# Squared-ReLU attention with a top-1 expert layer: another order of pairs in one chunk, later writes of transposed blocks, earlier v loads, two casts on another engine

## The chip, the cores and the metric

One core of a Trainium2 chip. The metric is the device time of one execution of the whole kernel in microseconds (us), as the median of several runs. Engines are named as the profile names them: PE (TensorE), DVE (VectorE), ACT (ScalarE), POOL (GpSimd) and SP (SyncE, whose queue issues nearly all DMAs here).

## The reference

Eight batches of 2496 tokens, 256 wide; z is 64 wide. Attention without a softmax, then a top-1 expert layer in which each of 8 experts takes at most 80 tokens.

```python
scores = (1.0 / S) * np.matmul(z, z.transpose(0, 2, 1))
attn = np.maximum(scores, 0.0) ** 2
x = (u * np.matmul(attn, v)).reshape(B * S, D)
logits = x @ w_gate                       # softmax, argmax: expert and gate weight of a token
...
h = np.maximum(x[tok_idx] @ w1[e], 0.0)   # the 80 tokens of largest gate weight for each expert
out[tok_idx] = gate_w[tok_idx, None] * (h @ w2[e])
```

The scores are symmetric: the block of rows i and columns j is the transpose of the block (j, i).

## The kernel before

The 2496 tokens of a batch are padded to NT = 20 tiles of 128. Four tiles make a chunk of 512 (NQ = 5 chunks), two tiles make a pair (NP = 10 pairs of keys). A step is one (batch b, query chunk qc, pair r): 50 steps for a batch, 400 in all, in the list `steps`. Chunks and pairs count from 0.

**A step on PE.** `attend` (L332) multiplies the 512 scores of two key tiles with v and accumulates over all pairs of the chunk in two PSUM banks (`acc`): for each tile and each half of D three matmuls, with v and the scores split in a high and a low part (L343 to L345); the last, half-filled tile k = 19 needs two (L347, L348). That makes 12 matmuls for a pair, 10 for the pair 9. `start` is given at k = 0, `stop` at the last tile.

**Where a step's scores come from.** `scores` (L303) is named LOOK = 2 steps ahead of `attend`. Either it computes them, when the key chunk is not below the query chunk: four matmuls (L312, L313) into PSUM, ReLU and square on ACT (L316, L317), the high part `ah` as a cast on ACT or DVE (`cp`, L105 or L107: DVE in the diagonal blocks and for the (chunk, tile) pairs in `ON_V`, from batch 1 on), the low part `al` as a subtraction on DVE (L54). Or, when the key chunk j is below the query chunk i, it takes the block (i, j) that an earlier chunk has computed, transposed (`mirrored`, L283): then ACT casts (L296) and DVE subtracts from a tile `blk`. Each chunk so begins with 2 qc mirrored pairs and ends with computed ones.

**How a block is mirrored.** `mirror` (L252) transposes 32 x 32 pieces of a computed tile on DVE into x (L257; four buffers), and after a block's fourth tile names the write of x to DRAM, y<-x (L261). `mirror_back` (L265), called at the end of each step, names the four reads blk<-y (L278) of the next block in the order of use, when its write is two or more steps back, its use is at most AHEAD = 12 steps away and one of NA = 4 slots is free. `to_read` holds each block's use step.

**What sets the order.** The order on PE, ACT, DVE and SP is the order in which the code names the instructions; each engine takes its own in that order. A DMA on SP that waits, for data or for a free buffer, holds all that is named after it on SP. In a step the order is: x of the finished chunk (at r = 0), `scores` of two steps ahead, v's preparation in batch 0, `attend`, `finished` (the rest for the chunk before: high, middle and low parts of x, its DMA transposes xq L412, its store xs L421 and L426, logits, gates), then the loads: z of the next batch (L100) at r = 1, the swapped z (zd, L120 and L121) at r = 1, u at r = 2, zeros to the output (L236) at r = 5, v (L132, two raw buffers), in batch 7 the expert weights (`weights_ahead`), at last `mirror_back`.

**v of the next batch.** Its groups 0 and 1 are loaded at pair 8 of chunk 3. In chunk 4, at pairs 2, 4, 6, 8 and 9, `prep_v` splits a group (cast on ACT L105, subtraction on DVE L146) and the load of the group after next is named. In batch 0 the same is done within chunk 0 at pairs 0, 2, 4 and 6.

After the attention comes the expert stage (from L798 on), which the change does not touch.

Of the kernel before, what the change touches and what calls it, by code (L numbers as in the profile page):

```python
# [8 lines left out]
F32 = mybir.dt.float32  # L9
# [16 lines left out]
def attn_moe_kernel(ctx, tc, zT, uT, v, wg, w1, w2, out, seq, cap):  # L26
# [5 lines left out]
    nc = tc.nc  # L32
    V = nc.vector
    B, _, SP = zT.shape
# [3 lines left out]
    NT = SP // P  # L38
# [3 lines left out]
    QT = 4  # L42
    NQ = NT // QT
# [9 lines left out]
    def tt(o, a, b, op):  # L53
        V.tensor_tensor(out=o, in0=a, in1=b, op=op)  # L54
# [9 lines left out]
    dram = ctx.enter_context(tc.tile_pool(name="dram", bufs=1, space=DRAM))  # L64
# [3 lines left out]
    SQ = 32  # L68
# [58 lines left out]
    def load_v(b, g):  # L127
        last = g == NQ - 1
        nf = QT - 1 if last else QT
        raw = zpool.tile([P, QT, D], F32, tag="vraw", name=f"vraw_{b}_{g}")  # L130
        r0 = g * CH
        nc.sync.dma_start(out=raw[:, :nf],  # L132
                          in_=v[b, r0:r0 + nf * P, :].rearrange("(t p) d -> p t d", p=P))
        if last:

            r1 = r0 + nf * P
            for h in range(2):
                nc.sync.dma_start(out=raw[h * 64:(h + 1) * 64, nf], in_=v[b, r1:r1 + TAIL, :])
        return raw
# [93 lines left out]
    def zero_out(i, n):  # L233
# [3 lines left out]
                          in_=zero.rearrange("p (o d) -> p o d", o=1).broadcast_to([P, r1 - r0, D]))  # L237


    LOOK, AHEAD = 2, 12  # L240
    a_t = {}

# [1 line left out]

    half_t, y_t, blk, slot_of, free = {}, {}, {}, {}, list(range(NA))
    n32 = P // SQ
    now = [0]

    to_read = [(b, i, j, ((b * NQ + i) * NT + j * QT) // 2 - LOOK)
               for b in range(B) for i in range(NQ) for j in range(i)]  # L250

    def mirror(b, i, j, t, a):  # L252

        if t == 0:
            half_t[b, i, j] = sqpool.tile([P, n32, QT, QT, SQ], F32, tag="x", name=f"x_{b}_{i}_{j}")
        x = half_t[b, i, j]
        V.transpose(out=x[:, :, :, t].rearrange("p n k s -> p k n s"), in_=a)  # L257
        if t < QT - 1:
            return
        y = dram.tile([n32, SQ, n32, QT * QT * SQ], F32, tag="y", name=f"y_{b}_{i}_{j}", bufs=12)  # L260
        nc.sync.dma_start(out=y.rearrange("g p h f -> (g p) (h f)"),  # L261
                          in_=x.rearrange("p h k t s -> p (h k t s)"))
        y_t[b, i, j] = y, now[0]

    def mirror_back():  # L265

# [15 lines left out]
    def pair_tile(tag, b, qc, k, dt=F32R, bufs=3):  # L282
        return ew.tile([P, 2, CH], dt, tag=tag, name=f"{tag}_{b}_{qc}_{k}", bufs=bufs)  # L283
# [17 lines left out]
    def scores(b, qc, k):  # L301

        if k // QT < qc:  # L303
            return mirrored(b, qc, k)
        nq = min(CH, seq - qc * CH)
        zc, zd = zc_t[b, qc], zd_t[b, qc]
        a = pair_tile("a", b, qc, k, F32, 2)
        ss = []
        for h in range(2):
            zk = zc_t[b, k // QT][:, (k % QT + h) * P:(k % QT + h + 1) * P]  # L310
            s = ps_s.tile([P, CH], F32, tag="s", name=f"s_{b}_{qc}_{k + h}")
            nc.tensor.matmul(s[:, :nq], zk, zc[:, :nq], start=True, stop=False)  # L312
            nc.tensor.matmul(s[:, :nq], zk, zd[:, :nq], start=False, stop=True)  # L313
            ss.append(s)
        for h, s in enumerate(ss):
            nc.scalar.activation(out=a[:, h, :nq], in_=s[:, :nq], func=AF.Relu)  # L316
        nc.scalar.activation(out=a[:, :, :nq], in_=a[:, :, :nq], func=AF.Square)  # L317
        ah = pair_tile("ah", b, qc, k)
        on_v = k // QT == qc or (qc, k) in ON_V and b > 0
        cp(V if on_v else nc.scalar, ah[:, :, :nq], a[:, :, :nq])  # L320
        al = pair_tile("al", b, qc, k)
        tt(al[:, :, :nq], a[:, :, :nq], ah[:, :, :nq], ALU.subtract)
        if k // QT > qc:
            for h in range(2):
                mirror(b, k // QT, qc, k % QT + h, a[:, h])
        a_t[b, qc, k] = (ah, al)
# [2 lines left out]

    def attend(b, qc, k, cols=range(DC)):  # L330
        nq = min(CH, seq - qc * CH)
        if k == 0:  # L332
            acc_t[b, qc] = [ps_a.tile([P, CH], F32, tag="acc", name=f"acc_{b}_{qc}_{c}")
                            for c in range(DC)]
        acc = acc_t[b, qc]
        ah, al = (x[:, k % 2, :nq] for x in a_t[b, qc, k - k % 2])
        vt = v_t[b, k // QT]
        t = k % QT
        for c in cols:
            cs = slice(c * P, (c + 1) * P)  # L340
            o = acc[c][:, :nq]
            if k < NT - 1:
                nc.tensor.matmul(o, vt[:, t, 0, cs], ah, start=k == 0, stop=False)  # L343
                nc.tensor.matmul(o, vt[:, t, 1, cs], ah, start=False, stop=False)  # L344
                nc.tensor.matmul(o, vt[:, t, 0, cs], al, start=False, stop=False)  # L345
            else:
                nc.tensor.matmul(o, vt[:, t, 0, cs], ah, start=False, stop=False)  # L347
                nc.tensor.matmul(o, vt[:, t, 0, cs], al, start=False, stop=True)  # L348


    xt_t, xq_t, lg_t = {}, {}, {}
# [256 lines left out]
        ts(pre["half"], incl[:, :, NBLK - 3], -15.5, ALU.add)  # L608


    NP = NT // 2

    ON_V = {(0, 8), (0, 12), (0, 16)}

    early = [(e, w, part) for e in range(2) for w in (1, 2) for part in range(2)]
    qa, qb, qz = NQ - 3, NQ - 2, NQ - 1
# [4 lines left out]
    WARM = 4, 12  # L621
    steps = [(b, qc, r) for b in range(B) for qc in range(NQ) for r in range(NP)]
    ET = mybir.EngineType
    v_raw, z_raw, w_raw = {}, {}, {}
# [68 lines left out]
    with tc.manual_schedule(engines={ET.PE, ET.Activation, ET.DVE, ET.SP}):  # L693
        prep_zc(0, 0, raw0)
        prep_zd(0, 0, raw0)
        prep_zc(0, 1, raw12[:, 0])
        scores(0, 0, 0)
        prep_v(0, 0, vraw0, nc.scalar, V)
        scores(0, 0, 2)
        v_raw[0, 1] = vraw1  # L700
        z_raw.update({(0, 2): raw12[:, 1], (0, 3): raw34[:, 0], (0, 4): raw34[:, 1]})
        constants()
        prev = None
        for i, (b, qc, r) in enumerate(steps):
            last = b == B - 1 and qc == NQ - 1
            now[0] = i
            if r == 0 and prev:
                chunk_x(*prev)
            if (b, qc) == (0, 0) and r in (0, 2, 4):
                prep_zc(0, r // 2 + 2, z_raw.pop((0, r // 2 + 2)))  # L710
            if i + LOOK < len(steps):
                nb, nqc, nr = steps[i + LOOK]
                scores(nb, nqc, 2 * nr)
            if b == 0 and qc == 0:
                if r % 2 == 0 and r < 8:
                    g = r // 2 + 1
                    prep_v(0, g, v_raw.pop((0, g)), nc.scalar, V)
                    if g + 1 < NQ:
                        v_raw[0, g + 1] = load_v(0, g + 1)
                if r == 8:  # L720
                    constants_v()
            for k in (2 * r, 2 * r + 1):
                if not last or k < NT - 3:
                    attend(b, qc, k)
            if prev:
                finished(*prev, r)

            nb, nqc = (b, qc + 1) if qc + 1 < NQ else (b + 1, 0)
            if r == 2:
                prep_u(b, qc)  # L730
            if b + 1 < B:
                if r == 1:
                    z_raw[b + 1, qc] = load_z(b + 1, qc)
                if r == 9:
                    prep_zc(b + 1, qc, z_raw.pop((b + 1, qc)))
                if qc == NQ - 2 and r == 8:
                    for g in range(2):
                        v_raw[b + 1, g] = load_v(b + 1, g)
                if qc == NQ - 1:
                    g = (r - 1) // 2 if r < 9 else 4  # L740
                    if r in (2, 4, 6, 8, 9):
                        prep_v(b + 1, g, v_raw.pop((b + 1, g)), nc.scalar, V)
                        if g + 2 < NQ:
                            v_raw[b + 1, g + 2] = load_v(b + 1, g + 2)
            if nb < B and r == 1:
                prep_zd(nb, nqc)
            if r == 5:
                zero_out(b * NQ + qc, B * NQ)
            if b == B - 1 and qc >= NQ - 3:
                weights_ahead(qc, r)  # L750
            mirror_back()
            if r == NP - 1:
                prev = b, qc

        chunk_tiles(*prev)
        for kk, c in ((3, 0), (2, 0), (3, 1), (1, 0), (2, 1), (1, 1)):
            attend(*prev, NT - kk, [c])
            if kk == 1:
                chunk_x_last(*prev, c)
        chunk_store(*prev)  # L760
        chunk_logits_last(*prev)
        gate_top(b, NQ - 1, NQ)
        gate(b, NQ - 1, NQ)
        chunk_store2(*prev)
        kb = B * BPB
        count_last(kb - 2, kb)
        blocks(ps_m, "m", gp, oh, kb - 2, kb)
# [546 lines left out]
```

## Time and profile before

| | |
|---|---|
| median of 3 runs | 1446.32 us (1445.33 to 1446.89) |
| the profiled execution | 1441.15 us, its span 1439.4 us |
| PE busy | 1385.3 us |
| DVE busy | 1074.9 us |
| ACT busy | 983.1 us |
| moved by DMA | 311.98 MB, mean 217 GB/s |
| mean granted clock of PE | 0.991 |

The profile's busy time of an engine is the union of its instructions' times, and a matmul's drawn length is longer than its slot in the pipeline, so that busy PE is not PE at its peak. A timeline row has start, length, engine, line, operation, out<-in, and in brackets the idle time of the engine before it with what ended it. A row of waits has the engine and instruction that waited, what it waited for, the total, the number of times and the longest. A row of windows has a stretch, its length, and the busy time of each engine with its number of instructions. For SP, a row is the time of issuing, not of the transfer. A row of DMA issues ends with the median time from issue to landing.

### The profile page before, as it was taken

How to read it: one execution, taken by the hardware profiler on the slowest of the kernel's cores; microseconds unless marked ns; L12 is line 12 of the kernel's file. 1: busy time of each engine (PE TensorE's matmuls, PEld its weight loads, DVE VectorE, ACT ScalarE, POOL GpSimd, SP SyncE). 2: the span in 40 equal slices, each digit the busy share in tenths (PEclk: the TensorE clock that was granted, in tenths of full speed). 3: DMA queues.
4: the chain of work that ended last, by engine and by line, in shares of the span. 5: the costliest groups of instructions: out<-in, count | busy, mean ns of one | idle time of the engine just before them, and what ended most of it. 6: DMA issues, size and time to landing. Idle time of an engine off the chain costs nothing. (4 is left out here: it accounts for less than half of the span.)

```text
span 1439.4 us, 19509 instructions
## 1 busy us (share of the span) xinstructions
PE 1385.3 (96%) x7086; PEld 1135.8 (79%) x7086; DVE 1074.9 (75%) x1530; ACT 983.1 (68%) x1263; POOL 47.5 (3%) x48
## 2 busy tenths in 40 slices
PE   8999999999999999999999999999999999999687
PEld 6788877888788887888788877888878888887466
DVE  7766788667877688677877678767887678766784
ACT  8776677767776587756676577766776667766264
POOL 0000000000000000000000000000000000000075
PEclk9999999999999999999999999999999999999899
DMA  6799978996999959997899959999598979999944
GB/s 203 207 227 223 242 198 209 239 243 157 236 247 222 251 157 216 263 213 210 232 210 237 241 156 235 240 230 259 152 233 237 240 159 238 235 231 253 207 147 134
DMA packets 300103, 311.98 MB, mean 217 GB/s; under 512 B 136184, under 2 KB 228224, under 8 KB 289760
## 3 DMA queue, kind: packets, MB, share of 16 engines
q1 hardware_dynamic: 299040, 309.11, 86.3%
q0 software_dynamic: 960, 1.56, 0.4%
q8 instruction: 57, 0.93, 0.3%
q14 instruction: 46, 0.38, 0.1%
HBM read 153.48 MB, written 126.46 MB: 194 GB/s over the span
## 5 line engine op out<-in xcount | busy, mean ns | idle before, releaser
L345 PE MATMUL acc<-al,vt 128*128 128x512 f32 (+1 forms) x1520 | 587.5, 386 | 7.3 <-DVE al L54 7.1
L343 PE MATMUL acc<-ah,vt 128*128 128x512 f32 (+1 forms) x1520 | 586.9, 386 | 6.3 <-ACT ah L296 4.0
L344 PE MATMUL acc<-ah,vt 128*128 128x512 f32 (+1 forms) x1520 | 586.0, 386 | 1.2 <-DVE vt L146 1.2
L54 DVE TENSOR_TENSOR al<-a,ah 128x1024 fp32r<-128x1024 f32 (+1 forms) x240 | 291.2, 1213 | 143.8 <-ACT ah L105 134.2
L345 PEld LDWEIGHTS acc<-al,vt 128*128 128x128 f32 x1520 | 285.7, 188 | 66.8 <-DVE al L54 14.4
L343 PEld LDWEIGHTS acc<-ah,vt 128*128 128x128 f32 x1520 | 285.8, 188 | 63.5 <-ACT ah L296 7.4
L344 PEld LDWEIGHTS acc<-ah,vt 128*128 128x128 f32 x1520 | 285.9, 188 | 55.1 <-DVE vt L146 2.0
L316 ACT ACTIVATE a<-s 128x512 f32<-128x512 f32 (+1 forms) x480 | 257.6, 588 | 83.1 <-PE s L313 73.4
L296 ACT CAST ah<-blk 128x1024 fp32r<-128x1024 f32 x160 | 166.9, 1048 | 163.0 <-DMA blk<-y 81.7
L54 DVE TENSOR_TENSOR al<-blk,ah 128x1024 fp32r<-128x1024 f32 x160 | 193.0, 1214 | 93.0 <-ACT ah L296 90.5
L317 ACT ACTIVATE a<-a 128x1024 f32<-128x1024 f32 (+1 forms) x240 | 253.0, 1054 | 7.6
L257 DVE STREAM_TRANSPOSE x<-a 128x512 f32<-128x512 f32 x320 | 207.6, 686 | 0.0
L313 PE MATMUL s<-zd,zc 128*128 128x512 f32 (+1 forms) x480 | 186.9, 389 | 0.0
L105 ACT CAST ah<-a 128x1024 fp32r<-128x1024 f32 x139 | 146.0, 1050 | 4.4
L312 PE MATMUL s<-zc,zc 128*128 128x512 f32 x320 | 131.3, 410 | 3.5 <-ACT a L316 3.4
L107 DVE CAST ah<-a 128x1024 fp32r<-128x1024 f32 (+1 forms) x101 | 68.6, 679 | 46.6 <-ACT a L317 46.6
L313 PEld LDWEIGHTS s<-zd,zc 128*128 128x128 f32 x480 | 90.4, 188 | 15.4 <-issue 0.5
L373 ACT CAST xb<-xf 128x1024 bf16<-128x1024 f32 (+1 forms) x39 | 40.1, 1027 | 57.3 <-DVE xf L362 57.2
L312 PEld LDWEIGHTS s<-zc,zc 128*128 128x128 f32 x320 | 60.1, 188 | 21.8 <-ACT a L316 11.8
L312 PE MATMUL s<-zc 128*128 128x512 f32 (+1 forms) x160 | 63.8, 399 | 7.7 <-ACT a L316 7.6
L146 DVE TENSOR_TENSOR vt<-vraw,vt 128x1024 fp32r<-128x1024 f32 (+1 forms) x40 | 46.7, 1167 | 27.8 <-ACT vt L105 27.6
L105 ACT CAST vt<-vraw 128x1024 fp32r<-128x1024 f32 (+3 forms) x56 | 44.9, 828 | 30.9 <-DMA vraw<-v 30.9
(161 smaller groups left out, 843.3 us busy)
## 6 DMA issues: line engine op xcount, KB each, us to landing
y<-x SPq DMA_DIRECT2D x80, 1024.0 KB, 5.4
blk<-y SPq DMA_DIRECT2D x320, 256.0 KB, 8.3
out<-idle SPq DMA_DIRECT2D x40, 512.0 KB, 9.3
vraw<-v SPq DMA_DIRECT2D x32, 512.0 KB, 8.4
ut<-uT SPq DMA_DIRECT2D x32, 512.0 KB, 5.4
xs<-xq SPq DMA_DIRECT2D x32, 512.0 KB, 7.6
wraw<-w SPq DMA_DIRECT2D x28, 512.0 KB, 6.1
zd<-zc SPq DMA_DIRECT2D x78, 128.0 KB, 3.5
```

Source lines behind the costliest of these rows:

```text
L54: V.tensor_tensor(out=o, in0=a, in1=b, op=op)
L105: eng.copy(out=o, in_=i)
L107: eng.tensor_copy(out=o, in_=i)
L257: V.transpose(out=x[:, :, :, t].rearrange("p n k s -> p k n s"), in_=a)
L296: nc.scalar.copy(out=natural(ah), in_=src)
L312: nc.tensor.matmul(s[:, :nq], zk, zc[:, :nq], start=True, stop=False)
L313: nc.tensor.matmul(s[:, :nq], zk, zd[:, :nq], start=False, stop=True)
L316: nc.scalar.activation(out=a[:, h, :nq], in_=s[:, :nq], func=AF.Relu)
L317: nc.scalar.activation(out=a[:, :, :nq], in_=a[:, :, :nq], func=AF.Square)
L343: nc.tensor.matmul(o, vt[:, t, 0, cs], ah, start=k == 0, stop=False)
L344: nc.tensor.matmul(o, vt[:, t, 1, cs], ah, start=False, stop=False)
L345: nc.tensor.matmul(o, vt[:, t, 0, cs], al, start=False, stop=False)
```

## The change

1. Chunk 3 (the fourth) takes its pairs in the order 8, 9, 0, 1, ..., 7, by a list `pairs_of`. `start` and `stop` of the accumulation, the use steps of the blocks and the look ahead follow that list. So the block (4, 3), which pairs 8 and 9 of chunk 3 compute, is computed first in the chunk.
2. `mirror` no longer names the write y<-x; it notes it, and `mirror_out`, called at the end of each step after `mirror_back`, names it two steps later.
3. The next batch's v groups 0 and 1 are loaded at pairs 2 and 4 of chunk 3 in place of both at pair 8.
4. `ON_V` keeps (0, 8) alone: the casts of chunk 0's tiles 12 and 16 go to ACT, in batches 1 to 7.

```diff
+    NP = NT // 2
+    pairs_of = [list(range(NP)) for qc in range(NQ)]
+    pairs_of[NQ - 2] = [NP - 2, NP - 1, *range(NP - 2)]
...
-    now = [0]
-    to_read = [(b, i, j, ((b * NQ + i) * NT + j * QT) // 2 - LOOK)
+    now, to_write = [0], []
+    to_read = [(b, i, j, (b * NQ + i) * NP + pairs_of[i].index(2 * j) - LOOK)
...
         if t < QT - 1:
             return
-        y = dram.tile([n32, SQ, n32, QT * QT * SQ], F32, tag="y", name=f"y_{b}_{i}_{j}", bufs=12)
-        nc.sync.dma_start(out=y.rearrange("g p h f -> (g p) (h f)"),
-                          in_=x.rearrange("p h k t s -> p (h k t s)"))
-        y_t[b, i, j] = y, now[0]
+        to_write.append((now[0], b, i, j, x))
+
+    def mirror_out():
+        while to_write and to_write[0][0] + 2 <= now[0]:
+            _, b, i, j, x = to_write.pop(0)
+            y = dram.tile([n32, SQ, n32, QT * QT * SQ], F32, tag="y", name=f"y_{b}_{i}_{j}", bufs=12)
+            nc.sync.dma_start(out=y.rearrange("g p h f -> (g p) (h f)"),
+                              in_=x.rearrange("p h k t s -> p (h k t s)"))
+            y_t[b, i, j] = y, now[0]
...
-        if k == 0:
+        first, last = 2 * pairs_of[qc][0], 2 * pairs_of[qc][-1] + 1
+        if k == first:
...
-    ON_V = {(0, 8), (0, 12), (0, 16)}
+    ON_V = {(0, 8)}
...
-                scores(nb, nqc, 2 * nr)
+                scores(nb, nqc, 2 * pairs_of[nqc][nr])
...
-            for k in (2 * r, 2 * r + 1):
+            p = pairs_of[qc][r]
+            for k in (2 * p, 2 * p + 1):
...
-                if qc == NQ - 2 and r == 8:
-                    for g in range(2):
-                        v_raw[b + 1, g] = load_v(b + 1, g)
+                if qc == NQ - 2 and r in (2, 4):
+                    g = r // 2 - 1
+                    v_raw[b + 1, g] = load_v(b + 1, g)
...
             mirror_back()
+            mirror_out()
```

More of the change, by code (lines that the diff above doesn't have):

```diff
@@ L342, in attend @@
             if k < NT - 1:
-                nc.tensor.matmul(o, vt[:, t, 0, cs], ah, start=k == 0, stop=False)
+                nc.tensor.matmul(o, vt[:, t, 0, cs], ah, start=k == first, stop=False)
                 nc.tensor.matmul(o, vt[:, t, 1, cs], ah, start=False, stop=False)
-                nc.tensor.matmul(o, vt[:, t, 0, cs], al, start=False, stop=False)
+                nc.tensor.matmul(o, vt[:, t, 0, cs], al, start=False, stop=k == last)
             else:
                 nc.tensor.matmul(o, vt[:, t, 0, cs], ah, start=False, stop=False)
-                nc.tensor.matmul(o, vt[:, t, 0, cs], al, start=False, stop=True)
+                nc.tensor.matmul(o, vt[:, t, 0, cs], al, start=False, stop=k == last)
     xt_t, xq_t, lg_t = {}, {}, {}
@@ L608, in half @@
         ts(pre["half"], incl[:, :, NBLK - 3], -15.5, ALU.add)
-    NP = NT // 2
-    ON_V = {(0, 8), (0, 12), (0, 16)}
+    ON_V = {(0, 8)}
     early = [(e, w, part) for e in range(2) for w in (1, 2) for part in range(2)]
```

## The prediction

> **What bounds the kernel now.** I read the page first (busy shares, then DMA), then windows of the span, then the waits of PE, and from there the timelines of ACT and SP in the stretches where PE stands.
>
> ```profile
> PE 1385.3 (96%) x7086; PEld 1135.8 (79%) x7086; DVE 1074.9 (75%) x1530; ACT 983.1 (68%) x1263; POOL 47.5 (3%) x48
> ...
> q1 hardware_dynamic: 299040, 309.11, 86.3%
> ```
>
> PE is the bound by its share, so nothing can gain that does not remove idle time of PE. The queue row says that the 16 DMA engines are close to full as well. The windows (length, then PE's busy time; the last three columns are granted clock, DMA share and GB/s) say where PE idles:
>
> ```profile
> 14.00:1347.00 1333.00, 1309.22 (x6635) 1080.17 (x6633) 1006.32 (x1341) 929.84 (x1175) 0.00 (x0) 1.00 0.90 221
> 38.00:50.00 12.00, 9.23 (x32) 6.89 (x32) 7.90 (x14) 6.67 (x10) 0.00 (x0) 0.86 0.98 289
> 344.80:380.90 36.10, 35.90 (x178) 28.71 (x176) 31.25 (x46) 27.40 (x38) 0.00 (x0) 1.00 0.66 189
> 415.40:479.70 64.30, 64.30 (x325) 52.78 (x324) 43.50 (x52) 41.58 (x51) 0.00 (x0) 1.00 0.99 227
> 1209.80:1224.10 14.30, 14.30 (x66) 11.56 (x65) 11.96 (x25) 10.88 (x15) 0.00 (x0) 1.00 0.94 232
> 1312.00:1346.00 34.00, 27.93 (x152) 22.89 (x151) 24.40 (x37) 18.30 (x23) 0.00 (x0) 1.00 0.99 248
> ```
>
> The attention loop (14 to 1347) has 1333.00 - 1309.22 = 23.8 us of PE idle. This understates what can be won, because a matmul is drawn longer than its slot:
>
> ```profile
> 22.42 0.39 PE L343 MATMUL acc<-ah,vt 128*128 128x512 f32 x1
> 22.65 0.39 PE L344 MATMUL acc<-ah,vt 128*128 128x512 f32 x1
> ```
>
> Starts are 0.23 us apart and each lasts 0.39, so every stall hides another 0.16. Chunks 2 and 3 of batch 2 (415.40 to 479.70) have no idle at all. Chunk numbers count from 0, so the "fourth chunk" is chunk 3. The idle sits in four places, and SP's queue stands behind most of it:
>
> ```profile
> SPq L261 <- DVE x L257: 324.1, 58, 16.4
> ```
>
> SP waits 324 us for the transposes that fill x, because the write y<-x is named as soon as the last transpose is, two pairs before DVE gets to it. All that follows on SP stands behind it.
>
> **Step A: the first chunk, v's last group.**
>
> ```profile
> 28.48 0.34 SPq L261 DMA_DIRECT2D y<-x  x1
> 28.91 3.58 SPq L278 DMA_DIRECT2D blk<-y  x4
> 32.59 0.45 SPq L132 DMA_DIRECT2D vraw<-v  x1
> ```
>
> ```profile
> 41.20 1.14 ACT L105 CAST vt<-vraw 128x768 fp32r<-128x768 f32 x2 [3.05 <-DMA vraw<-v]
> ```
>
> In the window 38 to 50 PE idles 12.00 - 9.23 = 2.8 us, and it has a granted clock of 0.86, another 0.14 x 12 = 1.7 us. The load of v's last group, issued at 32.59, lands 3.05 us after ACT wanted it. It stood behind a write of y (28.48) and four reads of blk. Renamed, that write and those reads come behind it in the queue; it can go as soon as its buffer is free, at least the 32.59 - 28.48 = 4.1 us earlier that those five took. 4.1 exceeds 3.05, so the whole 2.8 + 1.7 = 4.5 us goes. What is late next: nothing in that window, since the same steps of batch 2 (344.80 to 380.90) run with 0.2 us of idle.
>
> **Step B: the last chunk, pairs 6 and 7.** Seven windows, one for each of batches 0 to 6, from pair 5 to pair 9 of chunk 4; their sum:
>
> ```profile
> sum 110.50, PE 101.62 PEld 86.58 DVE 63.56 ACT 71.33 POOL 0.00; mean PE 14.52 PEld 12.37 DVE 9.08 ACT 10.19 POOL 0.00
> ```
>
> Idle is 110.50 - 101.62 = 8.9 us; with two stalls a window, 14 x 0.16 = 2.2 us are hidden, so 11.1 us. Batch 2 shows why, on SP and ACT:
>
> ```profile
> 477.47 0.34 SPq L261 DMA_DIRECT2D y<-x  x1
> 477.86 1.08 SPq L132 DMA_DIRECT2D vraw<-v  x2
> 485.57 1.75 SPq L278 DMA_DIRECT2D blk<-y  x4
> 487.42 6.49 SPq L412 DMA_TRANSPOSE xq<-xf  x2
> ...
> 496.48 0.41 SPq L132 DMA_DIRECT2D vraw<-v  x1
> ```
>
> ```profile
> 494.18 1.05 ACT L296 CAST ah<-blk 128x1024 fp32r<-128x1024 f32 x1 [4.67 <-DMA blk<-y]
> ...
> 503.00 1.05 ACT L105 CAST vt<-vraw 128x1024 fp32r<-128x1024 f32 x1 [4.02 <-DMA vraw<-v]
> ```
>
> The block (4,3) is computed by the last pairs of chunk 3, written at 477.47, read back from 485.57 on (SP waits for the write to land), and ACT needs it 4.67 us before it is there. While SP waits, the transposes of x, and behind them the load of v's third group (496.48), are late too, and ACT waits 4.02 us for that. The change has pairs 8 and 9 first, so their scores are named in chunk 2's pairs 8 and 9. By the code's conditions (write two pairs after, read at the second pair or later after that, in order, when a slot is free) the write of (4,3) is named at step 31 of the batch's 50 and the read at 35, for a use at 44; before it was 37 and 39. At 64.30 / 20 = 3.2 us a pair the read has 9 x 3.2 = 29 us instead of 16. The 4.67 goes. SP comes to the xq transposes without the stop from 477.86 + 1.08 = 478.94 to 485.57, and the third v group can go out up to 6.6 us earlier, which covers 4.02. The two loads moved to pairs 2 and 4 leave SP earlier as well (6 and 4 pairs, 19 and 13 us): their buffers have been free since the batch before, so they hold up no one, and ACT wants them only in chunk 4. I take 11.0.
>
> **Step C: chunk 0 to chunk 1, batches 1 to 6.** Six windows from pair 9 of chunk 0 to pair 3 of chunk 1, their sum; then ACT in batch 2:
>
> ```profile
> sum 95.90, PE 90.07 PEld 68.41 DVE 74.34 ACT 61.58 POOL 0.00; mean PE 15.01 PEld 11.40 DVE 12.39 ACT 10.26 POOL 0.00
> ```
>
> ```profile
> 377.50 0.34 ACT L467 ACTIVATE ex<-d 128x160 f32<-128x160 f32 x1 [3.07 <-DVE d L54]
> 378.52 2.00 ACT L296 CAST ah<-blk 128x1024 fp32r<-128x1024 f32 x2 [0.68 <-DMA blk<-y]
> ...
> 386.15 1.05 ACT L373 CAST xb<-xf 128x1024 bf16<-128x1024 f32 x1 [3.56 <-DVE xf L362]
> ```
>
> The same stretch of batch 7 takes 14.30 with no idle, so the six lose 95.90 - 6 x 14.30 = 10.1 us. Each has a first stall that comes with block (1,0) late (the 0.68 here) and a second with DVE late for xf (3.56); I put the first at two thirds. SP in batch 1:
>
> ```profile
> 190.41 0.35 SPq L261 DMA_DIRECT2D y<-x  x1
> ...
> 200.75 3.37 SPq L278 DMA_DIRECT2D blk<-y  x4
> ```
>
> ```profile
> y<-x SPq DMA_DIRECT2D x80, 1024.0 KB, 5.4
> ```
>
> The transposes xq and all else up to 200.75 stood behind the write at 190.41. Afterwards they go before it, the write goes at about its old time or 2 us later, and the read follows when the write has landed (median 5.4 us), at 196 to 198, some 3 us earlier than 200.75. That is more than the 0.68; the third that hangs on DVE I leave mostly standing. I take 7.5 of the 10.1.
>
> **The casts.** Two casts in each of batches 1 to 7 leave DVE for ACT, 14 in all.
>
> ```profile
> L105 ACT CAST ah<-a 128x1024 fp32r<-128x1024 f32 x139 | 146.0, 1050 | 4.4
> L107 DVE CAST ah<-a 128x1024 fp32r<-128x1024 f32 x85 | 58.6, 690 | 39.7 <-ACT a L317 39.7
> ```
>
> DVE is relieved of 14 x 0.69 = 9.7 us, ACT gets 14 x 1.05 = 14.7 us; these are the bounds, -9.7 and +14.7. In a chunk 0 of 36.10 us ACT goes from 27.40 to 29.5 and DVE from 31.25 to 29.9: neither binds. ACT has an idle 3.07 us before ex, more than the 2.1 us that it gets; but the subtraction behind each cast now waits for ACT, which eats DVE's relief. I take 0. If the cover before ex were gone, it would be the second rival. The Trainium skill speaks against this edit: in "ScalarE: Activation LUTs", section "Rules for kernel authors", simple elementwise work belongs on VectorE, which is faster for each element. The two rows agree on the price (1050 against 690 ns); by that rule alone the sum would be 14 x 0.36 = 5 us worse, an estimate.
>
> **Chunk 3's order.** Two scored pairs come two steps earlier than mirrored ones did. A scored pair takes PE 16 x 0.23 = 3.7 us and fits ACT and DVE there (41.58 and 43.50 us busy of 64.30). Where a run of scored pairs meets the end of a chunk, step C's third shows up to 0.5 us for each batch; so 0 to 8 x 0.5 = 4 us, and I take 0, because the next steps are mirrored and need no PSUM bank of PE.
>
> **Step D: batch 7, last chunk.** Idle 34.00 - 27.93 = 6.1 us. Part of it is block (4,3) and weight loads behind it on SP, part the splitting of weights itself, untouched. Half: 3.0.
>
> **Sum.** 4.5 + 11.0 + 7.5 + 3.0 = 26.0 us. The span of the profiled execution is
>
> ```profile
> span 1439.4 us, 19509 instructions
> ```
>
> and its time 1441.15 us (1.75 lie around the span), so 1415 for it; the median of the runs shown is 1446.32, 5.2 us more, and the forecast on that scale is 1446.3 - 26.0 = 1420.3, say 1420. Startup (before 14) and the expert stage (after 1347) are not touched.
>
> **The rivals.**
> Partial relief: SP stays behind for other reasons (the xq transposes alone hold it 6.49 us at 487.42), so v's third group and block (1,0) stay late. Then A 4.5 + half of B 5.5 + 3 of C and D = 13: 1433.
> ACT becomes the bound in chunk 0: the 14.7 us are exposed and C is lost. 4.5 + 11 + 3 - 14.7 = 4: 1442. Against it, 29.5 of 36.1 us.
> DMA is the real limit: engines at 0.90 to 0.99 of their time in the windows above; transfers moved ahead delay others, the waits change names, only A stays: 1442. For it, the share of 86.3%; against it, chunks 2 and 3 run at 0.99 with no PE idle. The Trainium skill ("DMA: Bandwidth & Descriptors", section "Specifications") gives about 358 GB/s from HBM for a core; by that figure 221 GB/s leaves room and this rival falls. The rows have the share at 0.99 with 227 GB/s, so I keep it.
> Slower: the writes are named two pairs later, and so are their reads (for block (2,1) from step 15 to 17 of a use at 20).
>
> ```profile
> 408.00 6.03 SPq L278 DMA_DIRECT2D blk<-y  x8
> ```
>
> ```profile
> 419.91 1.05 ACT L296 CAST ah<-blk 128x1024 fp32r<-128x1024 f32 x1 [5.74 <-DMA blk<-y]
> ```
>
> ACT already waits 5.74 us for (2,1), and PE just does not feel it. If the read really comes 2 x 3.2 = 6.4 us later, PE loses up to 6.4 us there in 8 batches and at (1,0) in 7: 15 x 6.4 = 96; with A, B and D's 18.5 gained, 1524. It decides from 18.5 / 15 = 1.2 us of delay a block on. Against it: SP now sits waiting for DVE before it can name the reads, so a later place in its program is not a later time.
>
> **How the numbers follow.** About 0.2% (2.9 us) is what a measurement of this kernel tells from no change. Forecast 0.72, its own range 1412 (all four places whole, 4.5 + 11.1 + 10.1 + 6.1 = 32, and the runs' spread) to 1428 (26 less the 4 us at chunk 3's edge and C by half); partial relief 0.10; DMA 0.08; ACT 0.05; slower 0.05. The range 1412 to 1434 takes in the first two, 0.82. Faster: 0.72 + 0.10 and 0.08 of the 0.13 at 1442 (0.3% below 1446.3), 0.90; within 0.2%: the other 0.05; slower: 0.05.
>
> **What would show it.** In the profile after: PE idle between 14 us and the end of attention about 4 to 8 us instead of 23.8; granted clock 1.00 around 40 us; SP's wait L261 for x far under 324 us; no ACT wait for blk in chunk 4 and none over 1 us for vraw; ACT's wait before ex under 1.5 us. I am wrong if ACT's wait for blk in chunk 2 passes 6 us and PE idles there, if new idle stands at the start of chunk 3, or if the DMA share rises and vraw still comes late.

## The result and the profile after

The changed kernel takes 1421.32 us (median of 4 runs, 1419.45 to 1422.23) where the kernel before, on the same chip, takes 1446.61 (1445.33 to 1448.48): a ratio of 0.9832, 95% interval 0.9809 to 0.9856. The forecast was 1420. One term of its sum, taken as 0, was nevertheless wrong by 9 us, and others that came out larger than predicted hid it. The profiled execution took 1419.45 us, 21.7 less than the profiled one of before; that is what the traces can explain.

The page of after, in the lines that answer to those shown of before:

```profile
span 1417.7 us, 19502 instructions
...
PE 1374.7 (97%) x7085; PEld 1136.9 (80%) x7086; DVE 1066.8 (75%) x1516; ACT 999.8 (71%) x1277; POOL 45.2 (3%) x48
...
q1 hardware_dynamic: 299040, 309.11, 88.4%
```

The bytes are the same, and the 16 DMA engines are now a larger share of a shorter span; PE's share rose too. The windows of after are, in order, the attention loop, the place of step A and the place of step D (length, busy times of PE, weight loads, DVE, ACT and POOL, then granted clock, DMA share, GB/s):

```profile
14.00:1325.00 1311.00, 1299.26 (x6637) 1081.69 (x6635) 998.17 (x1328) 947.01 (x1190) 0.00 (x0) 1.00 0.92 225
34.00:46.00 12.00, 12.00 (x54) 9.84 (x53) 10.32 (x19) 9.46 (x14) 0.00 (x0) 1.00 0.82 213
1293.70:1323.50 29.80, 26.56 (x149) 22.75 (x148) 22.60 (x34) 16.47 (x21) 0.00 (x0) 1.00 1.08 245
```

PE's idle time in the loop is 1311.00 - 1299.26 = 11.7 us, where before it was 23.8. Step A is won whole: 12.00 of 12.00 busy, and a clock of 1.00. Step D has 29.80 - 26.56 = 3.2 us idle instead of 6.1.

The same seven windows as step B (pair 5 to pair 9 of chunk 4, batches 0 to 6), then the same six as step C, each by its sum row:

```profile
sum 98.10, PE 98.00 PEld 87.76 DVE 63.89 ACT 66.23 POOL 0.00; mean PE 14.00 PEld 12.54 DVE 9.13 ACT 9.46 POOL 0.00
```

```profile
sum 87.20, PE 87.15 PEld 69.25 DVE 74.46 ACT 61.74 POOL 0.00; mean PE 14.53 PEld 11.54 DVE 12.41 ACT 10.29 POOL 0.00
```

B went from 110.50 to 98.10 us (12.4 won) with no idle left. C went from 95.90 to 87.20 (8.7 won).

So 4.5 + 12.4 + 8.7 + 2.8 = 28.4 us are won where the prediction looked, and the span is only 21.7 shorter, so at least 6.7 us are newly lost. The new loss stands at the third step of chunk 3, the first mirrored one there. Seven windows of after from the start of chunk 3 to just past that step, batches 0 to 6, one row and the sum:

```profile
443.60:454.00 10.40, 9.25 (x41) 7.32 (x40) 8.64 (x11) 5.01 (x6) 0.00 (x0) 1.00 1.11 263
...
sum 73.00, PE 64.94 PEld 51.40 DVE 60.62 ACT 35.28 POOL 0.00; mean PE 9.28 PEld 7.34 DVE 8.66 ACT 5.04 POOL 0.00
```

Idle is 73.00 - 64.94 = 8.1 us, and one stall a window hides 0.16 more: 9.2 us, 1.3 for each batch. Before, chunks 2 and 3 had next to no idle (0.15 us in all eight batches). The timelines of DVE, ACT and PE in after at this place (batch 2) show who is late:

```profile
445.51 1.30 DVE L262 STREAM_TRANSPOSE x<-a 128x512 f32<-128x512 f32 x2
446.73 0.38 DVE L112 CAST zc<-zraw 128x512 fp32r<-128x512 f32 x1
447.15 0.69 DVE L54 TENSOR_TENSOR zc<-zraw,zc 64x512 fp32r<-64x512 f32 x1
447.87 1.29 DVE L374 SCALAR_TENSOR_TENSOR xf<-acc,ut 128x512 f32<-128x512 f32 x2
449.07 1.22 DVE L54 TENSOR_TENSOR al<-blk,ah 128x1024 fp32r<-128x1024 f32 x1
```

```profile
444.24 1.04 ACT L307 CAST ah<-blk 128x1024 fp32r<-128x1024 f32 x1
449.19 1.04 ACT L385 CAST xb<-xf 128x1024 bf16<-128x1024 f32 x1 [3.91 <-DVE xf L374]
```

```profile
450.34 0.50 PE L357 MATMUL acc<-al,vt 128*128 128x512 f32 x1 [1.15 <-DVE al L54]
```

PE waits 1.15 us for the low part `al` of the first mirrored block. ACT had cast that block at 444.24, four us before. DVE comes to the subtraction at 449.07 only, after the transposes of the last computed pair, the preparation of the next batch's z (0.38 + 0.69) and the xf of the finished chunk (1.29). PE has little to do meanwhile: pair 9 has 10 matmuls instead of 12, and the scores named in that step are mirrored, so PE computes none. Batch 7, which has no next z to prepare, loses only 0.24 us there, counted from start to start of the matmuls (1.43 in batch 2); it loses another 0.6 at the next pair.

The waits on ACT and then on SP's queue in after (total, times, longest):

```profile
ACT ah L307 <- DMA blk<-y: 19.3, 9, 3.2
...
ACT vt L105 <- DMA vraw<-v: 9.4, 5, 3.8
```

```profile
SPq L289 <- DMA y<-x: 224.6, 38, 8.6
SPq L424 <- DVE xf L374: 121.2, 15, 11.8
SPq L424 <- DVE al L54: 90.0, 37, 7.7
SPq L272 <- DVE x L262: 52.0, 19, 9.6
```

SP's wait for x before it can write y fell from 324.1 to 52.0 us. SP is still not free: it now waits for a write to land before it can read back, 224.6 us in all, where before the row was

```profile
SPq L278 <- DMA y<-x: 47.7, 14, 6.7
```

These waits did not bring back the stalls at A, B and C. The batch 1 stretch that step C quoted now reads, on SP:

```profile
178.75 2.57 SPq L424 DMA_TRANSPOSE xq<-xf  x2
...
185.89 0.44 SPq L272 DMA_DIRECT2D y<-x  x1
...
193.34 1.74 SPq L289 DMA_DIRECT2D blk<-y  x4
```

The transposes xq go ahead of the write, as predicted, and the read goes at 193.34 instead of 200.75. Each edge starts a few us earlier now, so of those 7.4 us only a part was won at this place.

### The profile page after: what moved, and what is told of

It reads as the page before. It is cut to its first block, busy times and chain, and to the rows that moved or that the text cites. A ratio compares the mean times of both kernels' runs of the same rounds, so it can differ in the third digit from the quotient of the medians.

```text
span 1417.7 us, 19502 instructions
## 1 busy us (share of the span) xinstructions
PE 1374.7 (97%) x7085; PEld 1136.9 (80%) x7086; DVE 1066.8 (75%) x1516; ACT 999.8 (71%) x1277; POOL 45.2 (3%) x48
## 3 DMA queue, kind: packets, MB, share of 16 engines
q1 hardware_dynamic: 299040, 309.11, 88.4%
## 5 line engine op out<-in xcount | busy, mean ns | idle before, releaser
L105 ACT CAST ah<-a 128x1024 fp32r<-128x1024 f32 x153 | 160.7, 1050 | 4.8
L107 DVE CAST ah<-a 128x1024 fp32r<-128x1024 f32 (+1 forms) x87 | 59.1, 679 | 105.8 <-ACT a L328 105.5
L393 ACT CAST xb<-xr 128x1024 bf16<-128x1024 f32 (+1 forms) x39 | 40.0, 1025 | 27.9 <-DVE xr L54 27.4
L146 DVE TENSOR_TENSOR vt<-vraw,vt 128x1024 fp32r<-128x1024 f32 (+1 forms) x40 | 46.6, 1164 | 12.4 <-ACT vt L105 12.2
```

What stands on the lines that cost most here:

```text
L105: eng.copy(out=o, in_=i)
L107: eng.tensor_copy(out=o, in_=i)
```

## The experiments

The theory: the order puts block (4,3) ahead of its use, and the late write takes the stop out of SP's queue; the two together carry the gain, the v loads and the casts next to nothing, and the lost 9 us are DVE's order at chunk 3's third step. The rivals: one of the two parts alone carries all, or the v loads moved ahead do; and the new stall comes from a late block (a DMA) and not from DVE. The kernel before had medians from 1434.6 to 1440.0 us in the three sessions below, so the ratios, each taken on one chip, are compared and not the times.

**The order kept as before.**

```diff
-    pairs_of[NQ - 2] = [NP - 2, NP - 1, *range(NP - 2)]
```

> The change without its new order: chunk 3 takes its pairs 0 to 9 again; late writes, early v loads and moved casts stay. Theory 1 (the new order and the late write belong together): block (4,3) is now written at step 39, read at 41, used at 44, so a write and a read of together 13 us or more have about 8 us; PE loses some 4 to 6 us at pairs 6 and 7 of chunk 4 in each batch, while the idle that the changed kernel has at the third pair of chunk 3 (1.4 us in 7 batches) is gone: 1421 - 10 + 8 x 4 to 6 = 1443 to 1459. Rival (the order brings nothing, the late write brings it all): 1421 - 10 = 1411.

Measured: 1446.72 us against 1439.99, ratio 1.0054 (1.0033 to 1.0075): slower than before. (This run keeps the earlier v loads and the moved casts, and so does the next one.) The windows of step B in this kernel, its ACT timeline in batch 2, and its ACT waits:

```profile
sum 122.80, PE 106.63 PEld 90.83 DVE 68.30 ACT 76.95 POOL 0.00; mean PE 15.23 PEld 12.98 DVE 9.76 ACT 10.99 POOL 0.00
```

```profile
491.15 1.04 ACT L306 CAST ah<-blk 128x1024 fp32r<-128x1024 f32 x1 [7.87 <-DMA blk<-y]
```

```profile
ACT ah L306 <- DMA blk<-y: 54.4, 10, 7.9
```

Chunk 4 takes 122.80 us, 12.3 more than before. Without the new order, the late write makes block (4,3) later still: ACT waits up to 7.87 us where it waited 4.67. The stall in chunk 3 is gone in this kernel, and A and C are won (34.8 us for chunk 0 and 34.6 for chunk 1 in batches 1 to 6, from start to start, about as in the changed kernel). The late write without the order only moves the loss.

**The write at once.**

```diff
     mirror's end:
+        mirror_out()
...
-        while to_write and to_write[0][0] + 2 <= now[0]:
+        while to_write and to_write[0][0] <= now[0]:
```

> The change with the writes of blocks named at once, as before; new order, early v loads and moved casts stay. Theory 1 (SP's wait for the transposes holds up v in batch 0 and block (1,0) in batches 1 to 6): the idle there returns, 4.5 + 7.5 us, so 1433, with SP's wait for x in the hundreds of us again and a granted clock under 1 around 40 us; chunk 4 stays without idle. Rival (the order alone frees SP): 1421.

Measured: 1433.08 us, ratio 0.9953 (0.9936 to 0.9969). Its SP waits, its ACT waits and its windows of step C:

```profile
SPq L273 <- DVE x L262: 295.9, 57, 17.6
```

```profile
ACT ah L308 <- DMA blk<-y: 56.8, 22, 5.0
...
ACT vt L105 <- DMA vraw<-v: 22.5, 10, 3.0
```

```profile
sum 94.20, PE 89.94 PEld 68.44 DVE 74.43 ACT 61.58 POOL 0.00; mean PE 14.99 PEld 11.41 DVE 12.40 ACT 10.26 POOL 0.00
```

Without the late write, the order clears chunk 4 all the same: 29.05 us from start to start in each of batches 0 to 6, where before it took 30.04 to 31.76. It brings the stall in chunk 3, and leaves A and C much as they were: C stands at 94.20 (before 95.90), and SP's stop for x is back.

**The v loads late again; the casts on DVE again; and both.**

```diff
-                if qc == NQ - 2 and r in (2, 4):
-                    g = r // 2 - 1
-                    v_raw[b + 1, g] = load_v(b + 1, g)
+                if qc == NQ - 2 and r == 8:
+                    for g in range(2):
+                        v_raw[b + 1, g] = load_v(b + 1, g)
```

```diff
-    ON_V = {(0, 8)}
+    ON_V = {(0, 8), (0, 12), (0, 16)}
```

> The change with both v loads at pair 8 of chunk 3, as before. Theory 1: SP no longer stops in front of them, they land in time for pairs 2 and 4 of chunk 4, and the time is 1421 within 2 us. Rival (the early loads are what frees chunk 4): half of the 11 us of chunk 4 return, 1426 to 1432.

> The change with the casts of tiles 12 and 16 of chunk 0 on DVE again. Theory 1: neither engine binds there, 1421 within 2 us. Rival 1 (DVE's relief counts at the end of chunk 0): up to 1.38 us in 6 batches slower, 1424 to 1429. Rival 2 (ACT's added 14.7 us are exposed): 1407 to 1418.

> The change's new order and late writes alone: v loads at pair 8 and the casts of tiles 12 and 16 on DVE, as before. Theory 1 (these two parts are the whole effect): the changed kernel's time within 2 us. Rival (the loads and casts together carry a part that each alone hides): 3 to 8 us over it.

Measured: v late 1418.01 us, ratio 0.985 (0.9831 to 0.9868); casts on DVE 1419.41, 0.986 (0.984 to 0.988); order and late write alone, without the two other parts, 1418.27, 0.9849 (0.9829 to 0.9868). The changed kernel again, beside the last of these:

> The changed kernel itself, as the mark for the three beside it on this chip: 0.983 to 0.987 of the kernel before.

It took 1418.82, 0.985 (0.983 to 0.9869). The four can't be told apart. So the order and the late write are the whole effect that can be measured. Each has its own places: the order wins B and brings the new stall, the late write wins A and C. But the late write needs the order, because without it block (4,3) is later still. So the two do not simply add: 0.9953 and 1.0054, each without the other, would multiply to 1.0007, and together they give 0.9849.

**The new stall: z prepared earlier in chunk 2.** `prep_zc` goes from pair 9 to pair 7 there; nothing else changes. It was run beside the changed kernel and two other ways.

```diff
-                if r == 9:
+                if r == (7 if qc == NQ - 3 else 9):
```

> The changed kernel itself once more, as the mark for the kernels beside it: 0.983 of the kernel before, so 1415 to 1422 as this chip has the kernel before at 1440 to 1447.

> The changed kernel with one thing moved: in chunk 2 the next batch's z is prepared (two operations of DVE, 0.38 and 0.69 us) at pair 7 in place of pair 9. Theory 1 (the 1.4 us of idle at chunk 3's third pair come from DVE, which has z's preparation and x of the finished chunk between the last scored pair and the first mirrored one): the stall falls by 1.1 us in each of 7 batches, 1.4 to 0.3, and the time is 7 to 8 us under the changed kernel. Rival (ACT's wait for x, or PSUM, makes it): no change.

Measured: changed kernel 1415.76, 0.9865 (0.9845 to 0.9886); z earlier 1408.94, 0.9813 (0.9797 to 0.983). DVE's timeline at the same place of this kernel:

```profile
441.93 1.30 DVE L262 STREAM_TRANSPOSE x<-a 128x512 f32<-128x512 f32 x2
443.15 1.25 DVE L374 SCALAR_TENSOR_TENSOR xf<-acc,ut 128x512 f32<-128x512 f32 x2
444.33 1.20 DVE L54 TENSOR_TENSOR al<-blk,ah 128x1024 fp32r<-128x1024 f32 x1
```

The two rows of z are gone, the subtraction follows 2.40 us after the transposes' start instead of 3.56, and the stall falls from 1.43 us a batch to 0.25. The gain is 6.8 us in the medians; seven times 1.18 is 8.3. The rival cause, a late block, is out: no DMA was moved.

**The two heavy pairs third and fourth.**

```diff
-    pairs_of[NQ - 2] = [NP - 2, NP - 1, *range(NP - 2)]
+    pairs_of[NQ - 2] = [0, 1, NP - 2, NP - 1, *range(2, NP - 2)]
```

> The changed kernel with chunk 3 in the order 0, 1, 8, 9, 2 to 7: two mirrored pairs stand at the chunk's edge again, and block (4,3) is still written early (step 33, read from 35, used at 44). Theory 1: the idle at the third pair goes and chunk 4 stays free, 8 to 10 us under the changed kernel. Rival 1 (block (4,3) must come from the very first pairs): chunk 4's idle returns, up to 11 us over that, so about the changed kernel's time or more. Rival 2 (the stall follows the scored pairs wherever they stand): no change.

Measured: 1408.96, 0.9807 (0.9785 to 0.9829). The end of chunk 2 is light again, so the same DVE work costs nothing there, and about 0.25 us a batch are lost after the two heavy pairs. Chunk 4 still gets its block in time. In batch 7, 3.72 and 1.76 us are lost at pairs 6 and 7 of the last chunk, against 2.75 and 0 in the first trace of the changed kernel. That this is a price of the order is not shown: from start to start that chunk takes 33.19 us here, and 31.08, 29.27 and 32.95 in three profiled executions of the changed kernel itself.

**Both ends at once: a miss.** z earlier in chunk 2 and in chunk 0 as well, and at the start of chunk 3 the scores named ahead of x of the finished chunk.

```diff
-            if r == 0 and prev:
+            if r == 0 and prev and qc != NQ - 2:
                 chunk_x(*prev)
...
+            if r == 0 and prev and qc == NQ - 2:
+                chunk_x(*prev)
...
-                if r == 9:
+                if r == {0: 4, NQ - 3: 7}.get(qc, 9):
```

> The changed kernel's own order with DVE relieved at both edges: z prepared at pair 7 in chunk 2 and at pair 4 in chunk 0, and at the start of chunk 3 the mirrored pair's subtraction named ahead of x of the finished chunk. Theory 1: the 10 us at chunk 3's third pair go whole and the 0.25 us at chunk 1's second pair in 6 batches (1.5 us) too: 10 to 12 us under the changed kernel. Rival (ACT's wait for x): 0 to 3 us under it.

Measured: 1412.75, 0.9844 (0.9827 to 0.9862), 3 us under the changed kernel beside it. The first mirrored subtraction does go before xf, but the cast of xf on ACT then comes later, and the second mirrored block's cast stands behind it: the stall moved on by one pair, 0.81 us a batch there; batch 7 loses 1.94 over two pairs.

**The same without that swap.**

```diff
-                if r == 9:
+                if r == {0: 4, NQ - 3: 7}.get(qc, 9):
```

> The changed kernel with z prepared at pair 7 in chunk 2 and at pair 4 in chunk 0, x of the finished chunk where it was. Theory 1 (DVE at the chunk's edge): 1.4 us fall to 0.25 in 7 batches and the 0.25 us at chunk 1's second pair in 6 batches go, 9 to 10 us under the changed kernel. Rival (something else takes the place): 0 to 5 us under it.

Measured: 1409.58, 0.9793 (0.9772 to 0.9814), 9.2 us under the changed kernel of the same session (0.985). The start of chunk 3 in batch 2, and the attention loop:

```profile
440.70:449.90 9.20, 9.20 (x41) 7.31 (x41) 7.45 (x9) 4.99 (x6) 0.00 (x0) 1.00 1.06 260
```

```profile
14.00:1316.00 1302.00, 1298.46 (x6639) 1085.19 (x6637) 997.19 (x1330) 948.20 (x1189) 0.00 (x0) 1.00 0.91 227
```

The same 41 matmuls take 9.20 us where the changed kernel took 10.40, and 3.5 us of idle are left in the loop. This version beats both kernels.

**The slower rival, forced.** The writes named four pairs later instead of two.

```diff
-        while to_write and to_write[0][0] + 2 <= now[0]:
+        while to_write and to_write[0][0] + 4 <= now[0]:
```

> The changed kernel with the writes named four pairs later in place of two. Theory 1 (SP hardly waits for the transposes any more, so more delay only brings the reads nearer to their use; block (2,1) would be read at step 19 of a use at 20): PE loses 2 to 6 us there in each of 8 batches, 1432 to 1465 where the changed kernel has 1416. Rival (SP runs so far ahead of PE that its place in the program doesn't matter): no change.

Measured: 1537.29, 1.0675 (1.0651 to 1.0699), 118 us over the changed kernel, far outside what I had expected. Its waits, and SP and ACT in chunk 2 and at the end of chunk 3 of batch 2:

```profile
ACT ah L307 <- DMA blk<-y: 186.8, 28, 11.8
```

```profile
434.32 3.66 SPq L289 DMA_DIRECT2D blk<-y  x8
...
483.83 8.27 SPq L289 DMA_DIRECT2D blk<-y  x12
```

```profile
441.87 1.04 ACT L307 CAST ah<-blk 128x1024 fp32r<-128x1024 f32 x1 [11.64 <-DMA blk<-y]
...
491.93 2.00 ACT L307 CAST ah<-blk 128x1024 fp32r<-128x1024 f32 x2 [5.66 <-DMA blk<-y]
```

Block (2,1) is read at step 19 for step 20, and ACT waits 11.64 us for it; PE loses 5.8 to 8.3 us there in each of batches 1 to 7, 48 in all. Three blocks, which the changed kernel reads at steps 29 and 31, are all named at step 31 (the 12 reads at 483.83), the first of them for step 34. From start to start, about 1.5 us more are lost in chunk 3 in most batches and 15.5 in batch 7, and 4.2 to 7.5 in chunk 4 of batches 0 to 6. At a delay of two pairs none of this shows.

## Why the prediction was right, and where it was not

**A** was right in place, size and cause: the load of v's last group left SP at 26.33 us instead of 32.59, ahead of the write and the four reads, and the whole 4.5 us went. With the write at once most of A's loss is back (3.5 us by the starts of pairs 7 to 9), so it hangs on the late write.

**B** was right in its mechanism and a little small, 12.4 for 11.0. One reason that it gave is not needed: it counted on the next batch's v loads to leave SP earlier, and with these late again there is no stall in chunk 4 either. SP's stop for x is not what mattered: with the write at once SP waits 295.9 us for x, and batches 0 to 6 have no stall in chunk 4. What mattered is the order, by which block (4,3) is read at step 35 instead of 39 for its use at 44. Two of the signs did not come true: ACT waits over 1 us for vraw in three batches of the trace of after (3.77, 3.23 and 1.55), and twice for blk in chunk 4 (2.07 and 2.46). In batches 0 to 6 these waits cost PE 0.4 us in all.

**C** was 8.7 for 7.5. The first stall went, as argued; of the second, DVE late for xf, about 0.25 us is left at chunk 1's second pair in each of batches 1 to 6. With z prepared earlier in chunk 0 that goes too, so it has the same cause as the stall below.

**The casts** at 0: right, by the runs with and without them. But the sign that I named for it was wrong. ACT's wait before ex did not fall below 1.5 us; the row of after stands unchanged:

```profile
371.68 0.34 ACT L479 ACTIVATE ex<-d 128x160 f32<-128x160 f32 x1 [3.07 <-DVE d L54]
```

The rule of the Trainium skill ("ScalarE: Activation LUTs", "Rules for kernel authors"), which puts operations such as add and mul on VectorE and was read here as covering casts too, would have made the change 5 us worse, an estimate. The runs show 0.986 with them on DVE and 0.985 without, which can't be told apart: here the dearer instruction, on an engine that PE does not wait for, cost nothing that could be measured.

**Chunk 3's order, "I take 0": this step failed.** Its bound was 0 to 4 us; it measures 9.2 (10.5 when chunks 2 and 3 are counted from start to start of their matmuls). I weighed the two scored pairs by engine totals over two chunks (41.58 and 43.50 us busy of 64.30) and by PE's own time. The place where they meet the next step decides: after them come z's preparation, xf and the subtraction in one run on DVE, while PE has two short steps (2.72 and 2.27 us from start to start). The reason given, that the next steps are mirrored and need no PSUM bank of PE, was beside the point; mirrored steps still need DVE. The prediction did name new idle at the start of chunk 3 as what would show it wrong, and that is what stands there.

**D** was 2.8 for 3.0 by the trace of after. But batch 7's last chunk took 31.08 us in it and 29.27 and 32.95 in two other executions of the changed kernel, against 34.78 before, so a hit this close is chance.

The sum of the terms is 4.5 + 12.4 + 8.7 + 2.8 - 9.2 = 19.2 of the 21.7 us. Counted from the start of each step's first matmul to that of the next, the account of the two traces closes within 0.1 us: A 4.9, B 12.7, C 8.8, D 3.7, and 2.7 from small stalls in chunk 0 of batches 1 to 7, nearly all at its pairs 1 and 3, less 10.5 in chunks 2 and 3, come to 22.3 us. The attention starts 0.5 us later, and what follows it takes 0.2 more. The small stalls were not foreseen; they are shorter with either part of the change alone too. On the profiled execution the forecast of 1415 was 4.4 us too low, while the medians differ by 25.3 us, close to its 26.0. So the total came within 1.3 us partly by luck: B and C gave 2.6 us more than predicted, the rest of the trace 2.5, and the medians 3.6 more than the profiles, against 9.2 that were not foreseen. Idle in the loop is 11.7 us and not 4 to 8.

**The rivals.** Partial relief and ACT as the bound fell: C was won, and ACT's busy share went up by 3 points to no effect. DMA as the limit fell too. Its share rose to 88.4% while idle fell, and the new stall has a share of 1.11 in its window but ends on DVE. By its words one sign against the prediction came true, a larger DMA share with vraw still late; with 0.4 us of PE behind it, it does not bring this rival back. The slower rival is real as a mechanism and not at two pairs: it needed four. Block (2,1) then cost 48 us and block (1,0), also read one step before its use, nothing, where the prediction had 96 for the two; the rest of the 118 us stands where reads bunched up, in chunk 3 and chunk 4.

## What to carry to other kernels

A DMA that waits for its data stops everything named after it on its queue, so name it when its data are there, and check first how many steps are left between the read and the use; here two steps of delay cost nothing in the new order and 12 us in chunk 4 in the old one, and four steps cost 118. When heavy work is moved to another place in a loop, read the order of each engine over the few microseconds where it meets what comes next; shares over a chunk do not show a run of instructions on one engine. If the total fits the forecast, compare the terms all the same: here a loss of 9 us hid under it, and moving one small preparation by two pairs won 6.8 us of it back.

## What the runs showed of the hardware that was not expected

The same transfers take another time when they are named at another place. The rows of DMA issues of after (times, size of each, median us from issue to landing):

```profile
y<-x SPq DMA_DIRECT2D x80, 1024.0 KB, 8.1
blk<-y SPq DMA_DIRECT2D x320, 256.0 KB, 6.4
```

The write of y went from 5.4 to 8.1 us and the read of blk from 8.3 to 6.4, with the same bytes. This goes with the place of the write and not with the order: in the two kernels that name the write at once (before, and the new order with the write at once) the write took 5.4 and 5.6 us and the read 8.3 and 9.0; in all that name it later, 7.8 to 8.5 and 5.7 to 7.0. Why is not shown. A DMA share above 1, such as 1.11 at 263 GB/s, stands beside a PE that waits for DVE alone, so the share by itself does not show a limit.
